# Two-layer mixture behind a windowed attention: a new order for its beginning, and the last accumulator copied and stored in halves

## The chip, the cores and the metric

The kernel runs on one core of a Trainium2 chip. The metric is the device time of one execution in microseconds (us). The core has five engines that run their own instruction streams in order and wait for each other by semaphores: TensorE (PE in the rows, with its weight loads as PEld), VectorE (DVE), ScalarE (ACT), GpSimd (POOL) and SyncE (SP), which here issues every transfer between DRAM and the core's SBUF. Matmuls write to PSUM banks, which VectorE and ScalarE read.

## The reference

Attention in a window of 64 keys feeds a feed-forward layer with a squared ReLU, and that feeds one with x·cos(x).

```python
# q, k, v: (4, 8, 576, 64); moe_*: d_model 512, d_ff 2048; 2304 tokens
scores = scale * np.matmul(q, k.transpose(0, 1, 3, 2))
rel = pos[:, None] - pos[None, :]
scores = np.where((rel >= 0) & (rel < window), scores, -1e9)   # window 64
attn = softmax(scores)                       # exp(s - max) / (sum + 1e-9)
x = np.matmul(attn, v)                       # -> (2304, 512)
h = np.maximum(x @ w_in, 0.0);  x = h * h @ w_out          # first layer, weights w1
h = x @ w_in;                   out = h * np.cos(h) @ w_out   # second layer, weights w2
```

The weights are 8-byte floats. The kernel turns each 1 MB piece of them into a rounded fp32 high part and an fp32 remainder, and makes each matmul of three products (high·high, high·low, low·high).

## The kernel before

**Attention.** The 2304 tokens are nine blocks of 256, the heads two groups of four, so there are 18 attention units, named n_g (block, group). A unit loads `qk` and `v`, makes scores S (line 633, 32 matmuls), masks them and takes their maximum on VectorE (line 650), exponentiates them on ScalarE (line 656), normalises them on VectorE (line 666), transposes them in two halves T on TensorE (line 675), copies the halves to PT (line 301 or 305; `pb` for two units, by ScalarE or VectorE) and multiplies them by v to O (line 690, 32 matmuls). O becomes X, a high and a low part (lines 301, 305, 729).

**First layer.** The weights w1 come in 16 tiles: `raw_in_w1_dram_j` is loaded (line 330), converted by ScalarE (lines 341, 301) and VectorE (lines 353, 357) and split into `W` high (line 301 or 305) and `W` low (line 379, on VectorE or GpSimd). For each tile j, `ph` (line 1193) is 12 matmuls of X with W, `r` is its ReLU (line 772), `g` is r² in two parts (lines 776, 780, 785), and `accA` (lines 799, 860) adds 12 matmuls of g with the second half of W. The first 512 tokens are taken in two passes of 256 (128x256 tiles). `ph_i` runs two places ahead of the `accA` that takes g_i.

**Second layer's weights.** While the first layer runs, w2 tiles `raw_in_w2_dram_j` are loaded by the same line 330, converted to `cw` and from there split and combined into w2o, w2a and w2b, which are stored to DRAM. The second layer (from about 480 us on) reads them back and ends with accumulators `accB` (line 1042), which are copied to `o` (line 1056) and stored (line 1062).

**What sets the order.** Everything is declared as operations with the engines that could do them, a cost on each, a key and dependencies. `Plan.run` is a list scheduler that walks an estimated clock: among operations that could start first, it takes the lowest key, and books the engine. The order of each engine's instructions is that in which the plan took them; what an instruction really waits for is only its data and its buffers, and all behind it on its engine wait too. Keys and engines of the beginning come from the table `START`, searched offline against that estimate: `att` (key and spacing of a unit), `conv` (keys of conversion, split and load of the first nine tiles), `load` (keys of a unit's loads), `cast` and `low` (tiles whose split or low word VectorE may do too), `pool` (tiles whose `W` low GpSimd may do). A transfer costs SyncE in the estimate `max(0.6 * n, nbytes / 360e3)` us, and lands 2.2 us later. Where the plan sees TensorE wait, `keep_busy` puts in matmuls on a constant tile `still` (line 290), which write nothing that is used.

**Rings.** Raw tiles, W and w2 tiles share one ring of 18 slots in SBUF. `qk`, `v` and `PT` have one buffer each, so the next unit's `qk` can be loaded when the S before it is done, and its `v` when the O before it is done. SyncE issues in order, so a load behind these waits with them.

Of the kernel before, what the change touches and what calls it, by code (L numbers as in the profile page):

```python
# [16 lines left out]
P = 128  # L17
# [69 lines left out]
class Plan:  # L87
# [21 lines left out]
    def run(self):  # L109
        engines = sorted({e for o in self.ops for e in o.engs})  # L110
        free = dict.fromkeys(engines, 0.0)
        cand = {e: [] for e in engines}
# [74 lines left out]
def pe_us(n, passes=1):  # L187
# [5 lines left out]
START = {'ahead': 3,  # L193
          'att': {(0, 0): (-45.7, 5.7),
                  (0, 1): (-50.5, 14),
                  (1, 0): (-102.5, 14),
                  (1, 1): (-126.9, 4.1),
                  (2, 0): (7.3, 14),
                  (2, 1): (15.4, 9.4)},
          'cast': (0, 1, 2, 3, 4, 7, 9, 11, 12, 13),  # L200
          'conv': {0: (-8.4, 19.7, -47.8),
                   1: (-25.5, 11.0, -66.1),
                   2: (7.1, -30.3, -8.4),
                   3: (9.9, -33.5, -4.1),
                   4: (4.1, 8.7, -28.0),
                   5: (38.5, -3.6, 19.0),
                   6: (13.2, 7.2, 28.6),
                   7: (59.2, 17.9, -0.6),
                   8: (-4.2, 39.2, 23.5)},
          'diag': (),  # L210
          'exact': 3,
          'halves': 4,
          'load': {(0, 0): (-103.4, -79.0),
                   (0, 1): (-125.7, -51.9),
                   (1, 0): (-45.2, -57.1),
                   (1, 1): (-44.0, -53.5),
                   (2, 0): (19.6, 22.7),
                   (2, 1): (-5.1, 14.4)},
          'low': (0, 4, 5, 7, 9),
          'pool': (0, 1, 5, 6, 7, 9),  # L220
          'upper': ((0, 0), (0, 1), (1, 0), (1, 1), (2, 0), (2, 1))}
# [3 lines left out]
def kernel(  # L225
# [67 lines left out]
    def dma(key, fn, nbytes, deps=(), take=(), use=(), n=1, order=()):  # L293
        return op({"SP": max(0.6 * n, nbytes / 360e3)}, key, fn, [*deps, *order], take, use, lat=2.2)
# [727 lines left out]
    class Job:  # L1022
# [7 lines left out]
        def tile_op(self, m, key):  # L1030
# [22 lines left out]
            def cp_(e):  # L1053
                o["o"] = ma.tile([P, DM], F32, tag="x2", name=f"o_{p}_{half}_{m}")
                if e == "ACT":
                    nc.scalar.activation(o["o"], acc[0], AF.Copy)
                else:
                    nc.vector.tensor_copy(o["o"], acc[0])

            def st(e):  # L1060
                r0 = p * TW + half * H + m * P
                nc.sync.dma_start(out[r0:r0 + P, :], o["o"])
# [362 lines left out]
```

## Time and profile before

| | us |
|---|---|
| median of 3 runs | 857.79 |
| runs | 857.65, 857.79, 859.60 |
| profiled execution, its time | 857.64 |
| its span in the trace | 855.9 |
| outside the span | 1.74 |
| TensorE busy in the span | 843.2 (99%) |
| mean granted clock of TensorE | 0.995 of full speed |

The span is from the first to the last event of the profiled execution. TensorE is the engine with work nearly all the time, so a change of the time is a change of the stretches in which it waits or runs at a lower clock; what the other engines do counts where TensorE waits for it. Names in the trace drop the numbers of a tile: `raw_in_w_dram` is a raw tile of w1 or w2.

### The profile page before, as it was taken

The numbers are of one execution on the slowest core, as the hardware profiler recorded it, in microseconds if no ns is written. First come the engines' busy times: TensorE is split into PE (matmuls) and PEld (weight loads), VectorE is DVE, ScalarE is ACT, GpSimd is POOL, SyncE is SP. The second block draws the span as 40 slices with busy tenths as digits, with TensorE's granted clock in tenths as the row PEclk, the third lists the DMA queues.
The fourth block names the chain that finished last, engine by engine and source line by source line (L and its number), as shares of the span: only waits on it lengthen the run. The fifth ranks groups of instructions, "written<-read, shape, count | busy, mean of one in ns | idle before, by whom it ended". The sixth has DMA issues, their size and how long they took to land.

```text
span 855.9 us, 13984 instructions
## 1 busy us (share of the span) xinstructions
PE 843.2 (99%) x5248; PEld 737.3 (86%) x5248; DVE 574.6 (67%) x1348; ACT 514.0 (60%) x1090; POOL 10.7 (1%) x27
## 2 busy tenths in 40 slices
PE   7899999999999999999999999999999999999998
PEld 6798889998888888888888999988999988999986
DVE  6999666755656557543811688878688886788851
ACT  7799666756656666656433655564555563555542
POOL 3100000000000000000000000000000000000000
PEclk9899999999999999999999999999999999999999
DMA  8782334716445364543941297025453044643010
GB/s 346 309 330 92 103 119 187 288 53 240 188 174 203 142 228 151 177 192 124 337 192 37 86 397 280 13 93 240 183 199 124 1 158 174 231 150 124 1 38 37
DMA packets 28595, 144.16 MB, mean 168 GB/s; under 512 B 3056, under 2 KB 3568, under 8 KB 18288
## 3 DMA queue, kind: packets, MB, share of 16 engines
q1 hardware_dynamic: 28528, 143.27, 44.6%
q8 instruction: 41, 0.67, 0.3%
q14 instruction: 26, 0.21, 0.1%
HBM read 110.76 MB, written 32.51 MB: 167 GB/s over the span
## 4 chain that ended last, share of the span: by engine, by line
PE 94%; DMA 2%; DVE 2%; ACT 1%; issue 0%; POOL 0%; POOLq 0%; ACTq 0%; SPq 0%
PE accB L1042 23%; PE ph L1193 22%; PE accA L799 21%; PE x L1084 12%; PE z L1084 6%; PE y L1084 3%; PE O L690 2%; PE S L633 2%; PE T L675 2%; PE accA L860 1%; DMA w2a_dram<-w2a 1%; ACT pb L656 1%; DMA raw_in_w_dram<-in_w_dram 1%; DVE raw_in_w_dram L357 0%; DVE cw_in_w_dram L353 0%
## 5 line engine op out<-in xcount | busy, mean ns | idle before, releaser
L1193 PE MATMUL ph<-X,W_in_w_dram 128*128 128x512 f32 (+1 forms) x1008 | 215.7, 362 | 0.0
L799 PE MATMUL accA<-g,W_in_w_dram 128*128 128x512 f32 (+1 forms) x912 | 203.8, 370 | 0.0
L1193 PEld LDWEIGHTS ph<-X,W_in_w_dram 128*128 128x128 f32 x1008 | 170.3, 189 | 29.1 <-issue 1.2
L799 PEld LDWEIGHTS accA<-g,W_in_w_dram 128*128 128x128 f32 x912 | 157.7, 189 | 28.5 <-issue 1.5
L785 DVE TENSOR_TENSOR g<-r,g 128x512 fp32r<-128x512 f32 (+1 forms) x84 | 51.5, 614 | 95.2 <-ACT r L780 94.6
L1042 PE MATMUL accB<-wo,gb_e 128*128 128x512 f32 x432 | 100.1, 389 | 0.0
L1042 PEld LDWEIGHTS accB<-wo,gb_e 128*128 128x128 f32 x432 | 81.0, 188 | 16.6
L776 ACT ACTIVATE g<-r 128x512 fp32r<-128x512 f32 (+1 forms) x84 | 47.9, 570 | 73.9 <-PE accA L799 73.2
L772 ACT ACTIVATE r<-ph 128x512 f32<-128x512 f32 (+1 forms) x84 | 44.7, 532 | 42.4 <-PE ph L1193 41.5
L656 ACT ACTIVATE pb<-pb,mm 128x128 f32<-128x128 f32 x144 | 55.8, 390 | 14.9 <-DVE mm L650 14.8
L1042 PE MATMUL accB<-wo,gb_b 128*128 128x512 f32 x216 | 54.3, 393 | 0.0
L1042 PE MATMUL accB<-wo,gb_a 128*128 128x512 f32 x216 | 54.2, 393 | 0.0
L780 ACT ACTIVATE r<-r 128x512 f32<-128x512 f32 (+1 forms) x84 | 48.0, 571 | 2.6
L1042 PEld LDWEIGHTS accB<-wo,gb_b 128*128 128x128 f32 x216 | 40.2, 188 | 7.5
L1100 ACT ACTIVATE held<-x 128x384 f32<-128x384 f32 x72 | 34.4, 481 | 20.3 <-PE x L1084 20.3
L1042 PEld LDWEIGHTS accB<-wo,gb_a 128*128 128x128 f32 x216 | 40.2, 188 | 7.2
L1084 PE MATMUL x<-X,wb 128*128 128x384 f32 x216 | 45.7, 337 | 0.0
L1084 PE MATMUL x<-X,wa 128*128 128x384 f32 x216 | 45.3, 335 | 0.0
L353 DVE TENSOR_SCALAR cw_in_w_dram<-raw_in_w_dram 128x1024 int32<-128x1024 int32 x32 | 23.0, 721 | 30.6 <-ACT raw_in_w_dram L341 30.5
L341 ACT ACTIVATE raw_in_w_dram<-raw_in_w_dram 128x1024 f32<-128x1024 f32 x32 | 36.6, 1146 | 7.1 <-DMA raw_in_w_dram<-in_w_dram 7.1
L1084 PEld LDWEIGHTS x<-X,wa 128*128 128x128 f32 x216 | 38.7, 188 | 2.4
L1084 PEld LDWEIGHTS x<-X,wb 128*128 128x128 f32 x216 | 38.5, 188 | 0.3
(130 smaller groups left out, 1263.6 us busy)
## 6 DMA issues: line engine op xcount, KB each, us to landing
raw_in_w_dram<-in_w_dram SPq DMA_DIRECT2D x32, 1024.0 KB, 7.0
wa<-w2a_dram SPq DMA_DIRECT2D x24, 1024.0 KB, 7.1
wb<-w2b_dram SPq DMA_DIRECT2D x24, 768.0 KB, 5.8
qk<-in_qk_dram SPq DMA_DIRECT2D x17, 576.0 KB, 5.7
v<-in_v_dram SPq DMA_DIRECT2D x18, 512.0 KB, 3.7
w2o_dram<-w2o SPq DMA_DIRECT2D x8, 1024.0 KB, 4.0
w2a_dram<-w2a SPq DMA_DIRECT2D x8, 1024.0 KB, 5.0
wo<-w2o_dram SPq DMA_DIRECT2D x8, 1024.0 KB, 9.8
```

The costliest lines, as they stand in the source:

```text
L341: nc.scalar.activation(hw, hw, AF.Prelu, scale=2.0**-112, alpha=-(2.0**32))
L353: nc.vector.tensor_scalar(s["w"], words()[1], 3, None, ALU.logical_shift_left)
L656: nc.scalar.activation(t["pb"][:, e, r, i], t["pb"][:, e, r, i], AF.Exp, bias=t["mm"][:, e, r, i:i + 1], scale=-1.0, accum_out=t["sm"][:, ...
L772: nc.scalar.activation(t["r"], ph()[:, 0:w], AF.Relu)
L776: nc.scalar.activation(t["g"][:, 0], t["r"], AF.Square)
L780: nc.scalar.activation(t["r"], t["r"], AF.Square)
L785: nc.vector.tensor_tensor(t["g"][:, 1], t["r"], f32(t["g"][:, 0]), ALU.subtract)
L799: nc.tensor.matmul(self.acc[i][:, k, :], w[:, 1, wl, m * P:m * P + P], t["g"][:, gl, :], start=(j == 0 and p == 0 and k == 0 and self.n > ...
L1042: nc.tensor.matmul(acc[0], t["g"][:, gl, m * P:m * P + P], wb.tile[:, k % 2, wl], start=(k == 0 and i == 0), stop=(k == NJ - 1 and i == 2))
L1084: nc.tensor.matmul(ps[x], wb.tile[:, i, wl, c * P:c * P + P], piece(o, c, xl), start=(first and c == 0 and k == 0), stop=(last and c == 1 ...
L1100: return b, op({"ACT": act_us(H)}, key - 6, lambda e: nc.scalar.activation(r_at(b), ps[x], AF.Copy), [dep, o_rooms], [b], [buf], lat=0.39)
L1193: nc.tensor.matmul(t["ph"][:, 0:u.w], wb.tile[:, 0, wl, c * P:c * P + P], u.x(xl, c), start=(c == 0 and k == 0), stop=(c == NCC - 1 and k ...
```

## The change

The table `START` is replaced, with two numbers of the estimate that it was sought with: a load costs `nbytes / 400e3`, and SyncE's first transfer can begin at 0.7 us. Only tables and costs of the plan differ there, no operation of the computation. Work moves between the engines that may do it. The last accumulator `accB` is copied in two halves of 256 columns, one by ScalarE and one by VectorE, and each half is stored by itself; all other accumulators are copied and stored as before. In the new file a line is one further down (three after the last edit).

```diff
@@ class Plan: def run(self):
         free = dict.fromkeys(engines, 0.0)
+        free["SP"] = 0.7
@@ START (a few of its lines)
-          'conv': {0: (-8.4, 19.7, -47.8),
-                   1: (-25.5, 11.0, -66.1),
+          'conv': {0: (-8.3, 25.4, -70.8),
+                   1: (-12.2, -1.3, -83.6),
...
-          'low': (0, 4, 5, 7, 9),
-          'pool': (0, 1, 5, 6, 7, 9),
+          'low': (0, 2, 5, 6, 9),
+          'pool': (0, 1, 3, 5, 7, 11),
@@ def dma
-        return op({"SP": max(0.6 * n, nbytes / 360e3)}, key, fn, [*deps, *order], take, use, lat=2.2)
+        return op({"SP": max(0.6 * n, nbytes / 400e3)}, key, fn, [*deps, *order], take, use, lat=2.2)
@@ second layer, end of an accumulator
-            def cp_(e):
-                o["o"] = ma.tile([P, DM], F32, tag="x2", name=f"o_{p}_{half}_{m}")
-                if e == "ACT":
-                    nc.scalar.activation(o["o"], acc[0], AF.Copy)
-                else:
-                    nc.vector.tensor_copy(o["o"], acc[0])
-
-            def st(e):
+            def cp_(e, at):
+                if at.start == 0:
+                    o["o"] = ma.tile([P, DM], F32, tag="x2", name=f"o_{p}_{half}_{m}")
+                copy(e, o["o"][:, at], acc[0][:, at])
+
+            def st(e, at):
                 r0 = p * TW + half * H + m * P
-                nc.sync.dma_start(out[r0:r0 + P, :], o["o"])
-
-            c = op({"ACT": act_us(DM, False), "DVE": dve_us(DM)}, key - 8.0, cp_, [line[0]], [b],
-                   [acc[1]])
-            dma(key - 8.0, st, P * DM * 4, [c], use=[b])
+                nc.sync.dma_start(out[r0:r0 + P, at], o["o"][:, at])
+
+            end = (p, half, m) == (NPAIR - 1, 1, H // P - 1)
+            for k0, w, e in ((0, DM // 2, "ACT"), (DM // 2, DM // 2, "DVE")) if end else ((0, DM, None),):
+                at = slice(k0, k0 + w)
+                us = {"ACT": act_us(w, False), "DVE": dve_us(w)}
+                c = op({e: us[e]} if e else us, key - 8.0, lambda e, at=at: cp_(e, at), [line[0]],
+                       [] if k0 else [b], [b, acc[1]] if k0 else [acc[1]])
+                dma(key - 8.0, lambda e, at=at: st(e, at), P * w * 4, [c], use=[b])
```

The plan is walked anew as a whole, so the order changes far behind the beginning too: TensorE's order is the same again from about 135 us on, the other engines' keep small exchanges of neighbours up to the second layer. Three places follow.

**VectorE, about 20 us.** From the shift for the first weight tile on; `pb_1_0` is the block whose two transposes TensorE waits for there. Before:

```order
L353 TENSOR_SCALAR cw_in_w1_dram_0_371<-raw_in_w1_dram_0_209 128x1024
L662 TENSOR_SCALAR sm_1_0_353<-sm_1_0_353 128x4
L663 RECIPROCAL sm_1_0_353<-sm_1_0_353 128x4
L666 TENSOR_TENSOR pb_1_0_329<-pb_1_0_329,sm_1_0_353 128x512
L357 ISA raw_in_w1_dram_0_209<-raw_in_w1_dram_0_209,cw_in_w1_dram_0_371 128x1024x2
L662 TENSOR_SCALAR sm_1_0_353<-sm_1_0_353 128x4
L663 RECIPROCAL sm_1_0_353<-sm_1_0_353 128x4
L666 TENSOR_TENSOR pb_1_0_329<-pb_1_0_329,sm_1_0_353 128x512
L353 TENSOR_SCALAR cw_in_w1_dram_2_404<-raw_in_w1_dram_2_306 128x1024
L305 CAST W_in_w1_dram_0_417<-raw_in_w1_dram_0_209 128x2x512
```

In the change:

```order
L354 TENSOR_SCALAR cw_in_w1_dram_0_368<-raw_in_w1_dram_0_193 128x1024
L358 ISA raw_in_w1_dram_0_193<-raw_in_w1_dram_0_193,cw_in_w1_dram_0_368 128x1024x2
L663 TENSOR_SCALAR sm_1_0_353<-sm_1_0_353 128x4
L664 RECIPROCAL sm_1_0_353<-sm_1_0_353 128x4
L667 TENSOR_TENSOR pb_1_0_311<-pb_1_0_311,sm_1_0_353 128x512
L663 TENSOR_SCALAR sm_1_0_353<-sm_1_0_353 128x4
L664 RECIPROCAL sm_1_0_353<-sm_1_0_353 128x4
L667 TENSOR_TENSOR pb_1_0_311<-pb_1_0_311,sm_1_0_353 128x512
L306 COPY PT_1_0_404<-T_1_0_0_386 128x512
L730 TENSOR_TENSOR X_80<-O_0_0_333,X_80 128x2x256
```

Before, the first half of `pb_1_0` is normalised between the two conversions of tile 0 and the second behind them; in the change both conversions stand ahead of both. A PT copy and a low part of X follow, the `low` word of tile 2 comes to VectorE, and the high parts of W of tiles 0 and 2 go to ScalarE.

**SyncE, about 98 us.** From the v of unit 2_1 on. Before:

```order
L609 DMA v_2_1_1208<-in_v_dram 128x1024
L605 DMA qk_3_0_1218<-in_qk_dram 128x1152
L330 DMA raw_in_w2_dram_0_1291<-in_w2_dram 128x2048
L609 DMA v_3_0_1340<-in_v_dram 128x1024
L605 DMA qk_3_1_1349<-in_qk_dram 128x1152
L609 DMA v_3_1_1480<-in_v_dram 128x1024
L605 DMA qk_4_0_1490<-in_qk_dram 128x1152
```

In the change:

```order
L610 DMA v_2_1_1206<-in_v_dram 128x1024
L606 DMA qk_3_0_1215<-in_qk_dram 128x1152
L610 DMA v_3_0_1319<-in_v_dram 128x1024
L606 DMA qk_3_1_1328<-in_qk_dram 128x1152
L331 DMA raw_in_w2_dram_0_1351<-in_w2_dram 128x2048
L610 DMA v_3_1_1457<-in_v_dram 128x1024
L606 DMA qk_4_0_1466<-in_qk_dram 128x1152
```

The first w2 load stood behind qk_3_0 and ahead of v_3_0; now it stands behind v_3_0 and qk_3_1. These two wait for O of unit 2_1 and S of unit 3_0. On VectorE the shift of that tile stands ahead of the copy of the second half of PT_3_0 in both. Before:

```order
L353 TENSOR_SCALAR cw_in_w2_dram_0_1422<-raw_in_w2_dram_0_1291 128x1024
L305 COPY PT_3_0_1399<-T_3_0_1_1425 128x512
L357 ISA cw_in_w2_dram_0_1422<-raw_in_w2_dram_0_1291,cw_in_w2_dram_0_1422 128x2048
L305 CAST w2o_0_1458<-cw_in_w2_dram_0_1422 128x512
L409 TENSOR_TENSOR w2o_0_1458<-cw_in_w2_dram_0_1422,w2o_0_1458 128x512
```

In the change:

```order
L354 TENSOR_SCALAR cw_in_w2_dram_0_1404<-raw_in_w2_dram_0_1351 128x1024
L306 COPY PT_3_0_1378<-T_3_0_1_1399 128x512
L358 ISA cw_in_w2_dram_0_1404<-raw_in_w2_dram_0_1351,cw_in_w2_dram_0_1404 128x2048
L786 TENSOR_TENSOR g_17_1411<-r_17_1386,g_17_1411 128x512
L410 TENSOR_TENSOR w2o_0_1436<-cw_in_w2_dram_0_1404,w2o_0_1436 128x512
```

What moved around it is on TensorE: O of unit 3_0, which reads PT_3_0, stood behind all 12 matmuls of `ph_18` and 12 of `accA`; in the change it stands behind 6 of `ph_18`. O of 2_1 and S of 3_0 also stand earlier, by 9 matmuls of `accA` and 6 of `ph_17`.

**ScalarE, about 242 us.** From the conversion of the seventh w2 tile on. Before:

```order
L341 ACTIVATE raw_in_w2_dram_6_2805<-raw_in_w2_dram_6_2805 128x1024
L776 ACTIVATE g_44_2844<-r_44_2828 128x512
L780 ACTIVATE r_44_2828<-r_44_2828 128x512
L301 ACTIVATE raw_in_w2_dram_6_2805<-raw_in_w2_dram_6_2805 128x1024
L772 ACTIVATE r_45_2865<-ph_45_2840 128x512
L301 ACTIVATE PT_6_0_2809<-T_6_0_1_2860 128x512
L301 ACTIVATE X_80<-O_6_0_2878 128x2x256
```

In the change:

```order
L342 ACTIVATE raw_in_w2_dram_6_2796<-raw_in_w2_dram_6_2796 128x1024
L302 ACTIVATE raw_in_w2_dram_6_2796<-raw_in_w2_dram_6_2796 128x1024
L777 ACTIVATE g_44_2851<-r_44_2829 128x512
L781 ACTIVATE r_44_2829<-r_44_2829 128x512
L302 ACTIVATE w2o_3_2862<-cw_in_w2_dram_6_2842 128x512
L773 ACTIVATE r_45_2870<-ph_45_2844 128x512
L302 ACTIVATE PT_6_0_2810<-T_6_0_1_2864 128x512
L302 ACTIVATE X_80<-O_6_0_2879 128x2x256
```

The second conversion (line 302 of the change, raw from raw) now stands ahead of the two squares, and a copy of `cw_in_w2_dram_6` to w2o, which VectorE did before, stands ahead of the ReLU and the copy of PT_6_0.

## Rows read from the trace of the kernel before

**Rows 1.** Page: busy time, share of the span, instructions of an engine
```profile
PE 843.2 (99%) x5248; PEld 737.3 (86%) x5248; DVE 574.6 (67%) x1348; ACT 514.0 (60%) x1090; POOL 10.7 (1%) x27
```

**Rows 2.** Windows: busy (x) PE, PEld, DVE, ACT, POOL; clock, DMA share, GB/s
```profile
25.00:30.00 5.00, 4.43 (x49) 3.86 (x51) 4.90 (x7) 3.95 (x5) 2.72 (x1) 0.53 1.01 422
30.00:35.00 5.00, 5.00 (x57) 4.67 (x58) 4.96 (x20) 2.27 (x12) 0.61 (x1) 0.79 0.95 353
```

**Rows 3.** Timeline of TensorE, 20 to 38: start, duration, instruction, idle before
```profile
23.98 0.63 PE L675 MATMUL T<-ident,pb 128*128 128x128 f32 x4 [2.99 <-DVE pb L666]
...
26.14 1.08 PE L675 MATMUL T<-ident,pb 128*128 128x128 f32 x4 [0.57 <-DVE pb L666]
...
31.83 4.64 PE L1193 MATMUL ph<-X,W_in_w_dram 128*128 128x256 f32 x33
```

**Rows 4.** Timeline of GpSimd, 14 to 45
```profile
19.86 2.40 POOL L379 TENSOR_TENSOR W_in_w_dram<-raw_in_w_dram,W_in_w_dram 128x1024 fp32r<-128x1024 f32 x1 [13.32 <-ACT W_in_w_dram L301]
27.28 3.34 POOL L379 TENSOR_TENSOR W_in_w_dram<-raw_in_w_dram,W_in_w_dram 128x1024 fp32r<-128x1024 f32 x1 [5.01 <-DVE W_in_w_dram L305]
```

**Rows 5.** Timeline of VectorE, 14 to 45
```profile
21.18 1.64 DVE L353 TENSOR_SCALAR cw_in_w_dram<-raw_in_w_dram 128x1024 int32<-128x1024 int32 x1
...
25.91 0.69 DVE L353 TENSOR_SCALAR cw_in_w_dram<-raw_in_w_dram 128x1024 int32<-128x1024 int32 x1
...
28.37 2.80 DVE L305 CAST W_in_w_dram<-raw_in_w_dram 128x1024 fp32r<-128x1024 f32 x1
...
34.09 1.22 DVE L379 TENSOR_TENSOR W_in_w_dram<-raw_in_w_dram,W_in_w_dram 128x1024 fp32r<-128x1024 f32 x1
```

**Rows 6.** Timeline of SyncE's queue, 94 to 127
```profile
98.57 0.33 SPq L605 DMA_DIRECT2D qk<-in_qk_dram  x1
99.01 0.37 SPq L330 DMA_DIRECT2D raw_in_w_dram<-in_w_dram  x1
```

**Rows 7.** Line 330, loads issued from 95 to 260: issue to landing
```profile
DMA to landing us min/median/max: 4.7/7.1/8.4
```

**Rows 8.** Line 330, the load issued at 99.01: issue to landing
```profile
DMA to landing us min/median/max: 7.9/7.9/7.9
```

**Rows 9.** Timeline of TensorE, 94 to 124
```profile
109.56 1.10 PE L633 MATMUL S<-qk 64*64 64x128 f32 x32
...
112.08 2.90 PE L799 MATMUL accA<-g,W_in_w_dram 128*128 128x512 f32 x12
114.83 0.85 PE L1193 MATMUL ph<-X,W_in_w_dram 128*128 128x512 f32 x3
...
121.34 1.15 PE L690 MATMUL O<-PT,v 128*64 128x64 f32 x32
```

**Rows 10.** Timeline of VectorE, 108 to 123
```profile
120.05 0.69 DVE L305 COPY PT<-T 128x512 f32<-128x512 f32 x1 [0.76 <-PE T L675]
```

**Rows 11.** Timeline of ScalarE, 227 to 250
```profile
242.11 1.11 ACT L341 ACTIVATE raw_in_w_dram<-raw_in_w_dram 128x1024 f32<-128x1024 f32 x1 [2.98 <-DMA raw_in_w_dram<-in_w_dram]
...
244.31 1.12 ACT L301 ACTIVATE raw_in_w_dram<-raw_in_w_dram 128x1024 int32<-128x1024 uint32 x1
245.33 0.58 ACT L772 ACTIVATE r<-ph 128x512 f32<-128x512 f32 x1
245.81 0.58 ACT L301 ACTIVATE PT<-T 128x512 f32<-128x512 f32 x1
```

**Rows 12.** Timeline of VectorE, 227 to 250
```profile
245.47 1.22 DVE L357 CUSTOM_DVE_ANT_0 cw_in_w_dram<-raw_in_w_dram,cw_in_w_dram 128x2048 uint16<-128x2048 uint16 x1 [0.34 <-ACT raw_in_w_dram L301]
```

**Rows 13.** Timeline of TensorE, 227 to 250
```profile
246.45 1.15 PE L690 MATMUL O<-PT,v 128*64 128x64 f32 x30 [0.41 <-ACT PT L301]
```

**Rows 14.** Timeline of ScalarE, 849 to 858, the last copy
```profile
852.04 0.60 ACT L1056 ACTIVATE o<-accB 128x512 f32<-128x512 f32 x1 [1.49 <-PE accB L1042]
```

**Rows 15.** Line 1062, output stores issued from 845 on: issue to landing
```profile
DMA to landing us min/median/max: 2.0/2.0/2.3
```

**Rows 16.** Groups of ScalarE by form: busy, mean ns, idle before
```profile
L772 ACT ACTIVATE r<-ph 128x256 f32<-128x256 f32 x24 | 9.0, 376 | 3.5 <-PE ph L1193 2.7
```

More of the change, by code (lines that the diff above doesn't have):

```diff
@@ L188, in pe_us @@
     return max(0.108, 0.0134 + passes * n / 2400.0)
[L193 to L200, printed above, removed]
-          'conv': {0: (-8.4, 19.7, -47.8),
-                   1: (-25.5, 11.0, -66.1),
[L203 to L209, printed above, removed]
+START = {'ahead': 2,
+          'att': {(0, 0): (-23.1, 3.5),
+                  (0, 1): (-45.9, 14),
+                  (1, 0): (-116.4, 11.4),
+                  (1, 1): (-122.9, 14),
+                  (2, 0): (8.8, 12.4),
+                  (2, 1): (-6.3, 3.4)},
+          'cast': (3, 4, 6, 7, 9, 11, 14, 15),
+          'conv': {0: (-8.3, 25.4, -70.8),
+                   1: (-12.2, -1.3, -83.6),
+                   2: (0.8, -25.1, 1.9),
+                   3: (-1.3, -49.8, 5.6),
+                   4: (1.7, -4.9, -37.5),
+                   5: (38.9, 3.3, 27.3),
+                   6: (7.9, 9.0, 40.8),
+                   7: (62.6, 22.0, -5.5),
+                   8: (10.3, 36.0, 37.5)},
           'diag': (),
-          'exact': 3,
+          'exact': 5,
           'halves': 4,
[L213 to L218, printed above, removed]
-          'low': (0, 4, 5, 7, 9),
-          'pool': (0, 1, 5, 6, 7, 9),
-          'upper': ((0, 0), (0, 1), (1, 0), (1, 1), (2, 0), (2, 1))}
+          'load': {(0, 0): (-89.2, -90.6),
+                   (0, 1): (-140.3, -61.5),
+                   (1, 0): (-44.6, -41.1),
+                   (1, 1): (-39.2, -32.9),
+                   (2, 0): (8.8, 25.6),
+                   (2, 1): (6.3, 22.5)},
+          'low': (0, 2, 5, 6, 9),
+          'pool': (0, 1, 3, 5, 7, 11),
+          'upper': ((0, 1), (1, 0), (2, 0))}
 @with_exitstack
```

## The prediction

> **What bounds the kernel now.** The page comes first: TensorE is busy 843.2 of 855.9 us [rows 1], so at most some 13 us can be won, and anything that makes TensorE wait is paid in full. The windows of the beginning come next, since the list of TensorE's waits has all but one of them ahead of 31 us: there one sees the granted clock at 0.53 of full speed (its lower level, 1.2 GHz) from 25 to 30 and 0.79 as a mean from 30 to 35, while VectorE is busy 4.90 and 4.96 of 5 us [rows 2]. TensorE's timeline shows why it idled before: 2.99 us until the first transpose of unit 1_0, then again until the second at 26.14, both for a normalisation on VectorE; from 31.83 on it has work [rows 3]. So in the beginning VectorE sets the pace, and the clock fell behind the idle stretch. Behind that I read each place where the order differs, on the timelines of the engine that waits and of the one it waits for. One wait is left there, 0.41 us at 246.45 for a copy of PT by ScalarE [rows 13].
>
> **The beginning (term: -0.3 us).** VectorE had two operations of 0.69 us and more that took far longer than their like. The shift at 21.18 took 1.64 us against 0.69 for the one at 25.91, and the high part of W at 28.37 took 2.80 [rows 5]. Both lie beside GpSimd's low parts of W, 19.86 to 22.26 and 27.28 to 30.62 [rows 4], and both end 0.55 us behind them: VectorE's operation seems to run only when GpSimd's has ended. In the change, the two operations on X of unit 0_0 leave their place ahead of the masks, so the shift of tile 0 can begin at 21.18 - 2 x 0.6 = 20.0. But W low of tile 1 stays on GpSimd at about 19.7 to 22.1, so the shift ends at about 22.7 as before; and now the add of tile 0 (1.22, as in [rows 12]) stands ahead of the first normalisation. That one, with its two small steps of 0.4, ends at 24.9 and the second at 25.9. The first transpose moves from 23.98 to 25.0, the second from 26.14 to 26.0. TensorE idles 4.0 instead of 2.99 us, and the second transpose, which matters for O of 1_0, gains 0.1.
> Behind it VectorE had 0.6 + 0.6 + 1.2 + 2.8 us from 25.9 to the high part of X of 1_0 at 31.1. Now it has a copy of PT and a low part of X (0.6 each, from PSUM), the low word of tile 2 from about 27.2, which waits for GpSimd's W low of tile 0 to end (it can begin when ScalarE has W high, about 25.6, and takes 2.4: until 28.1, so the low word ends at 28.7), then shift and add of tile 2: 30.5. The chain that follows (X, eight masks, W low of tile 2 at 34.09 [rows 5], normalisations, transposes) is 0.6 earlier. TensorE's own chain at the lower clock (transpose, O, S, then 24 matmuls) is only 0.1 to 0.2 earlier. The gain is between the two, 0.15 to 0.6; I take 0.3. Bounds: 0.9 of gain if VectorE and GpSimd run beside each other; 0.4 of loss if the half clock slows what now stands behind a later transpose.
>
> **The first w2 load (term: +1.1 us).** Before, it was issued at 99.01, 0.44 behind qk_3_0 [rows 6], and landed 7.9 us later [rows 8], long before ScalarE read it. In the change it stands behind v_3_0 and qk_3_1, and qk_3_1 waits until S of 3_0 has read the only `qk` buffer. That S began at 109.56; 15 matmuls that stood ahead of it now follow. Twelve take 114.83 - 112.08 = 2.75 us with what lies between, or 0.23 each [rows 9], so S begins at 106.1, ends 1.1 later, qk_3_1 is issued at 107.3 and the w2 load at 107.7. Loads from here to 260 us landed in 4.7 to 8.4 us [rows 7]; with a v and a qk issued just ahead, as here, it was 7.9 [rows 8] or more. That gives 115.6 to 116.1. Then come ScalarE's conversion (1.1, as at 242.11 [rows 11]), VectorE's shift (0.7) and, queued behind the shift, the copy of the second half of PT_3_0 (0.69 [rows 10]): done at 118.1 to 118.6.
> O of 3_0 needs that copy. It began at 121.34, 10.7 us behind the end of S of 3_0 [rows 9], with 42 matmuls and two transposes between; now there are 39, which makes 10.0, so TensorE comes to it at 117.2. It waits 0.9 to 1.4 us: 1.1. Nothing covers this, since all of TensorE's later work is queued behind O. Bounds: no wait at all for a landing within 7.0 us, 1.4 at the slow end.
>
> **The seventh w2 tile (term: +0.8 us).** ScalarE converted at 242.11, then made two squares, the second conversion at 244.31, the ReLU at 245.33 and the copy of PT, which ended at 246.39 [rows 11]; O began behind it [rows 13]. The load of this tile depends on the same semaphores in both orders, so it should land where it did. In the change the second conversion goes from 243.1 to 244.25, VectorE's add behind it (1.22 [rows 12]) to 245.5, and ScalarE, which has its squares done by then, waits for the add, since the copy to w2o reads it. That copy costs 0.55, the ReLU 0.5, the copy of PT 0.58: 247.2 instead of 246.4. The add was beside this chain before and is now in it. So 0.8 us, bounds 0.6 and 1.0, and nothing if the tile lands over 1.3 us earlier.
>
> **Other moves (term: 0).** The first scores begin some 0.45 later behind two more pairs of constant matmuls, but ScalarE, whose exponentials set the pace there, has one copy less ahead of its first conversion, so that starts at the same time. The loads that are swapped at 260 us and later read buffers that are free earlier than TensorE wants them; W of tiles 5 and 8 is ready about 1 us before it is used. This 1 us is all their cover.
>
> **The tail (term: -0.1 us).** The last copy took 0.60 [rows 14]. ScalarE copies 256 columns in 0.376 [rows 16] while VectorE does the other half. The first store can go 0.2 earlier; the second follows on SyncE 0.44 behind (the distance of two issues in [rows 6]), so 0.2 later than the one store before. A store landed in 2.0 to 2.3 us [rows 15]. If half the bytes take as long, that is 0.2 lost; at 422 GB/s [rows 2] the half saved is 0.3 of flow, which gives 0.1 gained. I take 0.1 gained, bounds +0.25 and -0.3.
> [...]
>
> **Sum.** 857.64 - 0.3 + 1.1 + 0.8 - 0.1 = 859.1 us, against the profiled execution's own time, which is 0.15 below the median of the runs shown. About 2.6 us (0.3%) can be told from no change here, so this is no measurable change, on the slow side.
>
> **Rivals.** (1) The first w2 load lands in time, as the load with 4.7 us did: 858.0. For it speaks that the median is 7.1; against it the v and qk just ahead. (2) The beginning gets slower, and with it the kernel: the transpose comes 1 us later, the idle stretch is longer, and TensorE runs at the lower level for about 5 us more; at 0.53 that is 0.47 x 5 = 2.3 us, 861.4 in all. It decides from 1.3 us on, that is from 2.7 us more at the lower level. For it speaks that the clock fell behind an idle stretch of 2.99; against it that VectorE covers part of the loss. The Trainium skill, TensorE: Matmul & The Clock Gate, section What's actually happening, puts an idle engine back to 1.2 GHz; the trace agrees (0.53 behind the idle stretch [rows 2]). (3) The beginning gains much more: VectorE's operations aren't held by GpSimd, and TensorE keeps its full clock. The excess of the two long operations is 0.95 + 2.1 = 3.0 us, so at most that much goes: 859.1 + 0.3 - 3.0 = 856.4, and 855.3 if the load lands in time too. Against it speaks that both ended 0.55 us behind GpSimd's. (4) All the moves are covered: neither new wait shows, 857.2.
>
> **How the numbers follow.** Forecast 0.45 (own range 858.2 to 860.2), (1) 0.2, (2) 0.2, (3) 0.08, (4) 0.07. Slower by over 0.3% needs 860.4: nearly all of (2) and the slow edge of the forecast, 0.24. Faster needs 855.2: (3) with the load in time and the tail at its good end, 0.05. The rest is 0.71. The range runs from 856.8, between (3) and (4), to 861.2, short of the full price of (2).
>
> **What would show it.** VectorE's shift of tile 0 should begin near 20.0 and take over 2 us; TensorE's idle stretch before unit 1_0 should be about 4 us; the w2 load should be issued near 107.7 and TensorE wait about 1.1 us for VectorE's copy of PT at O of 3_0, and 1.2 for ScalarE's at O of 6_0 instead of 0.41. I am wrong if these waits are missing, if the windows up to 35 us show another clock, or if a wait stands at a place that I called covered.

## The result and the profile after

The changed kernel takes 862.95 us (median of 6 runs, 859.23 to 864.87) beside 858.25 for the kernel before (6 runs, 857.59 to 859.60): a ratio of 1.0051, 95% interval 1.0027 to 1.0074. It is slower by 0.5%, where I had forecast 859.1 us and no measurable change, with 861.2 as the upper end of the range. (Medians here and below are of all runs; ratios and their intervals leave out four slow runs of 929 to 3400 us and are not the quotients of the medians.) The profiled execution took 863.49 us (its span is 861.7), 5.85 more than the one profiled before, where the medians differ by 4.70. What follows explains those two executions; how far others repeat it is told with the experiments.

The busy times of TensorE and ScalarE are those of before to 0.1 us [rows 1], so the loss lies in waits.

```profile
PE 843.3 (98%) x5250; PEld 737.6 (86%) x5250; DVE 573.2 (67%) x1345; ACT 514.1 (60%) x1094; POOL 9.8 (1%) x27
```

The list of TensorE's waits (line, what it waited for, us in total, times, longest) names them. The second and third rows are to be looked at first: a second transpose that I had placed 0.1 us earlier than before waits 2.4, and O waits for ScalarE's copies of PT at two places, not at one.

```profile
PE T L676 <- DVE sm L663: 4.2, 2, 3.5
PE T L676 <- DVE pb L667: 2.8, 2, 2.4
PE O L691 <- ACT PT L302: 2.6, 2, 1.8
...
PE O L691 <- DVE PT L306: 0.7, 1, 0.7
```

**The beginning.** The timeline of TensorE, in the order of [rows 3]: matmuls of constants, first scores, the two transposes of unit 1_0, its O, and the first `accA`, the mark by which I measure the beginning.

```profile
1.19 4.89 PE L291 MATMUL S<-still 128*128 128x128 f32 x22 [1.19 <-DVE still L286]
6.01 1.54 PE L634 MATMUL S<-qk 64*64 64x128 f32 x48
...
20.45 1.61 PE L291 MATMUL T<-still 128*128 128x128 f32 x13 [0.59 <-issue]
25.53 0.63 PE L676 MATMUL T<-ident,pb 128*128 128x128 f32 x4 [3.47 <-DVE sm L663]
...
28.76 1.09 PE L676 MATMUL T<-ident,pb 128*128 128x128 f32 x4 [2.37 <-DVE pb L667]
...
31.06 1.98 PE L691 MATMUL O<-PT,v 128*64 128x64 f32 x32
...
39.89 1.31 PE L861 MATMUL accA<-g,W_in_w_dram 128*128 128x256 f32 x9
```

The same marks in the kernel before, of which no row was shown:

```profile
1.19 4.00 PE L290 MATMUL S<-still 128*128 128x128 f32 x18 [1.19 <-DVE still L285]
5.12 1.54 PE L633 MATMUL S<-qk 64*64 64x128 f32 x48
...
37.87 1.31 PE L860 MATMUL accA<-g,W_in_w_dram 128*128 128x256 f32 x9
```

The first `accA` is 2.02 us later. The first of the two waits is no surprise (I had said 4 us of idling; it is 3.47, and 0.59 more between the matmuls on constants ahead of it). The second is, and the timelines of VectorE and GpSimd of the changed kernel, which answer to [rows 4, 5], show what it is:

```profile
20.39 2.71 DVE L354 TENSOR_SCALAR cw_in_w_dram<-raw_in_w_dram 128x1024 int32<-128x1024 int32 x1
...
24.70 0.69 DVE L667 TENSOR_TENSOR pb<-pb,sm 128x512 f32<-128x512 f32 x1
...
25.71 2.90 DVE L667 TENSOR_TENSOR pb<-pb,sm 128x512 f32<-128x512 f32 x1
...
29.74 0.68 DVE L308 TENSOR_SCALAR raw_in_w_dram<-raw_in_w_dram 128x1024 int32<-128x1024 uint32 x1
```

```profile
20.15 2.41 POOL L380 TENSOR_TENSOR W_in_w_dram<-raw_in_w_dram,W_in_w_dram 128x1024 fp32r<-128x1024 f32 x1 [13.57 <-DMA v<-in_v_dram]
25.68 2.40 POOL L380 TENSOR_TENSOR W_in_w_dram<-raw_in_w_dram,W_in_w_dram 128x1024 fp32r<-128x1024 f32 x1 [3.11 <-ACT W_in_w_dram L302]
```

GpSimd's second low part of W begins at 25.68, the second normalisation at 25.71. The normalisation, 0.69 us of work, ends 0.53 behind GpSimd, as the shift ahead of it ends 0.54 behind the first low part. I had expected the operation held there to be the low word at 29.74; it came through in 0.68. In the kernel before, the second normalisation had no low part of GpSimd beside it:

```profile
25.30 0.69 DVE L666 TENSOR_TENSOR pb<-pb,sm 128x512 f32<-128x512 f32 x1
```

**O of three units.** On TensorE's timeline each O now comes in two pieces: two matmuls, then the wait for the copy of the second half of PT, then 30. At the first and second of these places the kernel before had no such wait ([rows 9], and the first row below); at the third it had 0.41 [rows 13]. At the second it had the copy of PT on VectorE. Before:

```profile
206.39 1.15 PE L690 MATMUL O<-PT,v 128*64 128x64 f32 x32
```

```profile
205.10 0.69 DVE L305 COPY PT<-T 128x512 f32<-128x512 f32 x1 [1.08 <-PE T L675]
```

In the change:

```profile
119.30 0.33 PE L691 MATMUL O<-PT,v 128*64 128x64 f32 x2
120.37 1.15 PE L691 MATMUL O<-PT,v 128*64 128x64 f32 x30 [0.74 <-DVE PT L306]
...
209.72 0.33 PE L691 MATMUL O<-PT,v 128*64 128x64 f32 x2
210.86 1.15 PE L691 MATMUL O<-PT,v 128*64 128x64 f32 x30 [0.81 <-ACT PT L302]
...
250.15 0.33 PE L691 MATMUL O<-PT,v 128*64 128x64 f32 x2
252.26 1.15 PE L691 MATMUL O<-PT,v 128*64 128x64 f32 x30 [1.78 <-ACT PT L302]
```

What a wait displaces is the distance of the two pieces less about 0.07 for two matmuls: 1.0 at unit 3_0, 1.07 at 5_0, 2.04 at 6_0, of which 0.67 stood there before, so 1.37. With the beginning that is 2.02 + 1.0 + 1.07 + 1.37 = 5.46 of the 5.85. The rest, 0.4, I did not place; 0.3 of it is there by O of 5_0, to which TensorE comes 3.33 us later than before (209.72 instead of 206.39).

ScalarE's timeline answers to [rows 11]. At unit 5_0 the copy of PT stands behind both conversions of the fifth w2 tile, whose load landed at 207.66 (the first row waited for it). At unit 6_0 it stands behind both conversions, two squares and the copy to w2o.

```profile
207.67 1.13 ACT L342 ACTIVATE raw_in_w_dram<-raw_in_w_dram 128x1024 f32<-128x1024 f32 x1 [1.04 <-DMA raw_in_w_dram<-in_w_dram]
208.70 1.13 ACT L302 ACTIVATE raw_in_w_dram<-raw_in_w_dram 128x1024 int32<-128x1024 uint32 x1
...
210.19 0.61 ACT L302 ACTIVATE PT<-T 128x512 f32<-128x512 f32 x1
...
247.14 1.13 ACT L342 ACTIVATE raw_in_w_dram<-raw_in_w_dram 128x1024 f32<-128x1024 f32 x1 [3.56 <-DMA raw_in_w_dram<-in_w_dram]
...
250.61 0.63 ACT L302 ACTIVATE w2o<-cw_in_w_dram 128x512 fp32r<-128x512 f32 x1
...
251.62 0.59 ACT L302 ACTIVATE PT<-T 128x512 f32<-128x512 f32 x1
```

**The tail.** The chain of waits, at its end, has ScalarE's half and VectorE's half one behind the other, not side by side:

```profile
857.87 0.39 ACT o L302
858.26 0.02 issue
858.28 0.42 DVE o L306
```

From the start of ScalarE's copy to the end of the span it is 861.7 - 857.87 = 3.83 us, and before 855.9 - 852.04 = 3.86 [rows 14]. In this pair of executions the tail gains 0.03 us.

### The profile page after: what moved, and what is told of

Read it like the earlier page. It is cut to its first block, busy times and chain, and to the rows that moved or that the text cites. A ratio compares the mean times of both kernels' runs of the same rounds, so it can differ in the third digit from the quotient of the medians.

```text
span 861.7 us, 13997 instructions
## 1 busy us (share of the span) xinstructions
PE 843.3 (98%) x5250; PEld 737.6 (86%) x5250; DVE 573.2 (67%) x1345; ACT 514.1 (60%) x1094; POOL 9.8 (1%) x27
## 4 chain that ended last, share of the span: by engine, by line
PE 92%; DMA 3%; ACT 2%; DVE 2%; issue 0%; SPq 0%; ACTq 0%
PE accB L1043 23%; PE ph L1196 21%; PE accA L800 20%; PE x L1087 12%; PE z L1087 6%; PE y L1087 3%; DMA raw_in_w_dram<-in_w_dram 2%; PE O L691 2%; PE S L634 2%; PE T L676 1%; PE accA L861 1%; DMA w2a_dram<-w2a 1%; ACT pb L657 1%; PE S L291 1%; DVE pb L667 0%
```

## The experiments

Theory 1 after this reading: the loss is the order's alone, and consists of four places: the second normalisation of unit 1_0 that runs beside GpSimd's low part (called the collision below), and the copies of PT at O of 3_0, 5_0 and 6_0. Theory 2, its rival, is named with each run. In the diffs below `behind(a, b, ...)` takes b, ... out of the written order and puts them right behind a, and `before` right ahead of it; nothing else of the plan changes. All times are medians, beside the kernel before run with them (857.70 us for the first four, 858.27 for shift32, gps_wait2, best_after and best_before, 858.40 for gps_look, 857.94 for nine_first, best_after9 and best_before7).

**order_only.** The changed kernel with the tail of before.

```diff
-                copy(e, o["o"][:, at], acc[0][:, at])
+                if e == "ACT":
+                    nc.scalar.activation(o["o"], acc[0], AF.Copy)
+                else:
+                    nc.vector.tensor_copy(o["o"], acc[0])
...
-                nc.sync.dma_start(out[r0:r0 + P, at], o["o"][:, at])
+                nc.sync.dma_start(out[r0:r0 + P, :], o["o"])
```

> The new table and the two new costs alone; the last accumulator is copied and stored whole, as before. Theory 1 (the loss is made by the new order, in the beginning and at three copies of PT): within 1 us of the change, about 863, and the same waits of TensorE in its trace: about 6.5 us in all for transposes ahead of 31 us, 0.7 at 120, 0.8 at 211 and 1.8 at 252. Theory 2 (the two halves of the tail cost something by themselves): about 858 to 860, nearer to the kernel before.

Measured: 862.70 us, ratio 1.0047 (1.0027 to 1.0067). The order alone makes the loss; the halves of the tail neither add nor save what can be told.

Its trace doesn't repeat all the sizes that I expected. The waits at O of 3_0 and 5_0 are 0.68 and 0.89, but the one at 6_0 is 0.67, not 1.8. A further one of 1.22 stands at 173 us, for a ReLU on ScalarE behind the two conversions of a w2 tile, whose load ScalarE waited for 2.43 us there and 0.74 in the profiled changed kernel:

```profile
173.23 1.70 PE L1194 MATMUL ph<-X,W_in_w_dram 128*128 128x256 f32 x12 [1.22 <-ACT r L773]
...
253.97 1.15 PE L691 MATMUL O<-PT,v 128*64 128x64 f32 x30 [0.67 <-ACT PT L302]
```

In the five traces of the new order that leave the three places as they are (the changed kernel, called after here and in the table below, order_only, gps_wait, gps_look, nine_first) TensorE idles 0 to 0.74 us at O of 3_0, 0 to 0.95 at 5_0 and 0.67 to 2.31 at 6_0. So the three sizes above are those of one execution.

**waits_off.** The changed kernel with three moves back: the first w2 load ahead of v_3_0, and at the fifth and seventh w2 tile the second conversion and the add (with the copy to w2o at the seventh) behind the copy of PT. (In the names, `c1` is the second conversion, `add` VectorE's add behind it, `w2o` and `w2ol` the copy to w2o and its low part; the last number of a PT is its half.)

```diff
+        before(("v", 3, 0), ("load", "in_w2_dram_0"))
+        behind(("PT", 5, 0, 1), ("c1", "in_w2_dram_4"), ("add", "in_w2_dram_4"))
+        behind(("PT", 6, 0, 1), ("c1", "in_w2_dram_6"), ("add", "in_w2_dram_6"), ("w2o", 3, 0), ("w2ol", 3, 0))
```

> The change, with three operations moved in the written order: the first w2 load stands ahead of v_3_0 again; the copies of PT_5_0 and PT_6_0 on ScalarE stand ahead of the second conversion of their w2 tile, and of the copy to w2o. Theory 1 (each of the three waits is made by that order): TensorE's waits at 120, 211 and 252 are gone or under 0.3 us each, and the time falls by about 3.4, to 860. Theory 2 (late w2 transfers make them, whatever the order behind them): the first wait goes, the other two stay at half or more, about 861.5.

Measured: 859.60 us, ratio 1.0014 (1.0004 to 1.0025), 3.35 below the changed kernel and 3.1 below order_only, with which it ran. The three places were moved together, so what each is worth by itself was not measured. The list of TensorE's waits of this run ends with the beginning; no O waits any more, while the wait for the normalisation stays:

```profile
PE T L702 <- DVE sm L689: 5.0, 2, 4.3
PE T L702 <- DVE pb L693: 2.4, 2, 2.0
PE S L660 <- DVE mm L677: 2.0, 1, 2.0
PE S L311 <- DVE still L306: 1.2, 1, 1.2
```

**gps_wait.** GpSimd waits with its low part of tile 0 until the second normalisation is done, by a copy of 8 columns of its result to a new small tile.

```diff
+    hold = cp.tile([P, 8], F32, name="hold")
...
+            if j == 0 and e == "POOL":
+                nc.gpsimd.tensor_copy(hold[:, 0:8], watch["pb"])
```

> The change, with one edit: GpSimd reads 8 columns of the second normalised half of pb_1_0 ahead of its low part of W of tile 0, so that this part starts behind that normalisation instead of 0.03 us ahead of it. Theory 1 (VectorE's operations from SBUF to SBUF wait while GpSimd computes a low part): the normalisation takes 0.7 instead of 2.90, the second transpose comes near 26.5 instead of 28.76, and the time falls by about 2, to 861. Theory 2 (VectorE is held by the transfers, which run at full rate there): the normalisation stays long, no change. Theory 3 (the lower clock makes the loss, not the wait): the transpose comes earlier, but the first accA still starts at 39.5 or later.

Measured: 866.49 us, ratio 1.0095 (1.0080 to 1.0110): slower than the changed kernel, not faster. The beginning alone did what theory 1 says. On VectorE's timeline the normalisation is short again, and the operation that is held now is the low word, which has time:

```profile
25.70 0.69 DVE L695 TENSOR_TENSOR pb<-pb,sm 128x512 f32<-128x512 f32 x1
...
27.51 2.14 DVE L326 TENSOR_SCALAR raw_in_w_dram<-raw_in_w_dram 128x1024 int32<-128x1024 uint32 x1
```

The second transpose came at 26.54 instead of 28.76 and the first `accA` at 38.22 instead of 39.89. Then the gain was lost all along the first layer: twelve matmuls to `ph` of 512 columns took 2.96 us there, 2.88 to 2.91 in the changed kernel. The new tile had moved all later ones of the pool by 32 bytes.

**all_fixed.** waits_off and gps_wait together, with a tile of its own for each half of the last output.

```diff
+                o[at.start] = ma.tile([P, DM], F32, tag="x2", name=f"o_{p}_{half}_{m}_{at.start}")
+                copy(e, o[at.start][:, at], acc[0][:, at])
```

> The change with the edits of both other runs, and with a tile of its own for each half of the last accumulator, so that the second copy need not wait for the first. Theory 1: all the losses found are gone: 0.3 gained in the beginning, 0.4 at the wait that the kernel before had at 246, 0.4 in the tail, so 856.8 against 857.6 for the kernel before. Theory 2 (something not seen yet costs time): 858 or more.

Measured: 863.15 us, ratio 1.0055 (1.0040 to 1.0070). It has the same shift of 32 bytes in it, so its time says nothing against theory 1; its beginning repeats gps_wait's (first `accA` at 38.34). VectorE's half still began 0.23 behind the end of ScalarE's, now waiting for an earlier store from its buffer, so whether the halves can run side by side was not shown.

**shift32.** The kernel before with an unused tile of 32 bytes.

```diff
     still = cp.tile([P, 2, P], F32, name="still")
+    cp.tile([P, 8], F32, name="spare")
```

> The kernel before with a tile of 32 bytes a partition that nothing uses, ahead of the weights' ring in SBUF. No instruction is added or moved. Theory 1 (matmuls of the first layer run slower when their operands are moved by 32 bytes): 12 matmuls of ph take 2.80 instead of 2.72 us and the time is 4 to 5 us more, about 862. Theory 2: no change, 857.7.

Measured: 862.43 us, ratio 1.0044 (1.0028 to 1.0060). The groups of TensorE by form (busy us, mean ns) put most of it at the matmuls to `ph` of 512 columns. The kernel before, then shift32:

```profile
L1193 PE MATMUL ph<-X,W_in_w_dram 128*128 128x512 f32 x720 | 176.1, 392 | 0.0
```

```profile
L1194 PE MATMUL ph<-X,W_in_w_dram 128*128 128x512 f32 x720 | 179.8, 397 | 0.0
```

That is 3.7 beside the 4.2 us by which the medians differ; of the second layer's `accB` one group grew by 1.5 and another shrank by 0.7. An experiment that adds a tile must put it where nothing moves.

**gps_wait2** and **gps_look.** gps_wait with the 8 columns copied to a small tile that the kernel has already, so that nothing moves. gps_look is the same kernel, traced once more.

```diff
-    edge.tile([P, 8], F32, name="edge")
+    hold, watch = edge.tile([P, 8], F32, name="edge"), {}
```

> The same edit of the change as in gps_wait (GpSimd's W low of tile 0 behind the second normalisation of pb_1_0), but its 8 columns go to a small tile that was there already, so that no other tile moves in SBUF. Theory 1 (VectorE waits for GpSimd; the loss of gps_wait came from the 32 bytes by which its new tile moved the tiles behind it): the normalisation takes 0.7, the first accA starts near 38.2, 12 matmuls of ph take 2.72 us again, and the time is about 861.5. Theory 2 (the later W low itself made the rest slower): 865 or more again.

> The same kernel as gps_wait2, whose one trace showed a whole execution at the lower clock and can't be read. Theory 1 (the collision of the second normalisation of unit 1_0 with GpSimd's low part of W delays the beginning; the price of the 32 bytes is separate): normalisation at 25.7 of 0.69 us, second transpose at about 26.5 instead of 28.76, first accA at about 38.2 instead of 39.89, twelve ph in 2.88 (not 2.96), time 861 to 862, about 1 us below the changed kernel. Theory 2 (the beginning is late for another reason, later dummies or the clock): first accA still at 39.5 or later though the transpose comes early.

Measured: gps_wait2 861.99 us, ratio 1.0037 (1.0020 to 1.0054); gps_look 861.23, ratio 1.0032 (1.0021 to 1.0043). So the wait of GpSimd gains 1.0 to 1.7 us on the changed kernel by the medians, but the intervals overlap that of the changed kernel (1.0027 to 1.0074), so the times alone do not decide. The trace of gps_look seems to speak for theory 2, with the first `accA` at 39.95. But all of its beginning stands 0.7 us or more later from the first exponential on (8.30 instead of 7.59), and the windows show the lower clock in a stretch where the profiled changed kernel had none. (Columns as in [rows 2].)

```profile
10.00:15.00 5.00, 4.37 (x37) 4.12 (x38) 3.88 (x21) 4.80 (x24) 0.00 (x0) 0.66 1.00 390
```

From there on I compared all traces by three marks, read from their timelines:

| kernel | first exponential | first `accA` | between | clock 10 to 15 us | collision |
|---|---|---|---|---|---|
| before | 6.70 | 37.87 | 31.17 | 1.00 | |
| shift32 | 7.19 | 38.36 | 31.17 | 1.00 | |
| after | 7.59 | 39.89 | 32.30 | 1.00 | yes |
| waits_off | 7.25 | 39.47 | 32.22 | 1.00 | yes |
| gps_wait | 7.59 | 38.22 | 30.63 | 1.00 | no |
| all_fixed | 7.70 | 38.34 | 30.64 | 1.00 | no |
| order_only | 8.07 | 41.21 | 33.14 | 0.66 | yes |
| gps_look | 8.30 | 39.95 | 31.65 | 0.66 | no |
| best_after | 8.18 | 39.77 | 31.59 | 0.66 | no |

Behind the first exponential the beginning is as good as fixed. The collision costs 1.6 to 1.7 us at the full clock (32.22 and 32.30 against 30.63 and 30.64) and 1.5 at the lower (33.14 against 31.65 and 31.59). Without it the new order is 31.17 - 30.63 = 0.54 faster than the old one. The lower clock at 10 to 15 us goes with 0.8 to 1.0 more in this distance, and comes in some executions of the old order too (0.67 and 0.71 in the last two kernels below). And the first exponential itself comes later in the new order (7.25 to 8.30, against 6.70 and 7.19).

**best_after.** order_only with gps_wait2 and waits_off: the new order without the four places.

> The new table and costs with the tail of before, with the edits of gps_wait2 and waits_off, so without the three waits and without the collision at the normalisation. Theory 1 (these four are the whole loss): 857.5 to 858, level with the kernel before, because the new beginning then ends 0.3 later than the old one (38.2 against 37.87 for the first accA) and 0.6 is won at the wait that the kernel before has at 246. Theory 2 (the new table also costs elsewhere): 859 or more.

Measured: 858.39 us, ratio 0.9999 (0.9985 to 1.0013), level with the kernel before. The four places make the whole loss, to about 1 us. (This kernel also lacks the 0.7 us that the kernel before loses at O of 6_0 [rows 13], so the rest of the new order may still cost about that much.) Its profiled execution is its slowest (861.88), and the wait at 172 us that order_only had is 2.19 in it:

```profile
171.83 1.69 PE L1225 MATMUL ph<-X,W_in_w_dram 128*128 128x256 f32 x12 [2.19 <-ACT r L804]
```

The kernel before and the profiled changed kernel have no wait there. So a w2 load that lands later makes part of the difference between executions of one kernel.

**nine_first** and **best_after9.** The first scores stand behind 11 matmuls of constants, where the order before had 9 (22 and 18 rows above). Back to 9, in the changed kernel and in best_after:

```diff
+        next(o for _, o in order if o.pre).pre = 9
```

> The changed kernel with 9 matmuls of constants ahead of its first scores, as before the change, instead of 11. In the traces so far the first exponential of the new order stands at 7.25 to 8.30 us, that of the old at 6.70 to 7.46, and from there to the first accA it is a fixed distance (31.17 in the old order, 32.2 to 32.3 in the new at full clock). Theory 1: the two matmuls delay the scores, and all of the beginning with them: first scores at 5.1 to 5.4 instead of 6.01, first exponential at 6.7 to 7.2, and the kernel is 0.7 to 0.8 us faster, 862.2. Theory 2: the scores wait for the load of qk in either case, or something behind them gives the time back: no change, 862.9.

> The new order without its three later waits and without the collision at unit 1_0 (best_after, which was level with before), now with 9 matmuls of constants ahead of the first scores instead of 11. Theory 1: 0.7 to 0.8 us faster than best_after, 857.6, ratio about 0.999; from the first exponential to the first accA 30.6 us at full clock. Theory 2: no change, 858.4.

Measured: nine_first 860.78 us, ratio 1.0031 (1.0019 to 1.0043), but best_after9 858.33, ratio 1.0001 (0.9992 to 1.0010). The first is more than I expected, with an interval that overlaps the changed kernel's; the second is nothing. In both traces the scores began at 5.33 as expected, but took 2.0 us instead of 1.54, so the first exponential came at 7.41 and 7.39. The clock was at 0.68 from 10 to 15 us, and from the first exponential on they agree with the table's rows for that clock: 33.26 us to the first `accA` with the collision, 31.65 without it. What two matmuls of constants cost in the end stays open.

**best_before** and **best_before7.** The kernel before with what was learnt: GpSimd's low part of tile 0 waits for VectorE's high part of tile 2, and the copy of PT of 6_0 goes ahead of the second conversion, the add and the copy to w2o; then the same with 7 matmuls of constants first.

```diff
+        behind(("Whi", 2), ("Wlo", 0))
+        behind(("PT", 6, 0, 1), ("c1", "in_w2_dram_6"), ("add", "in_w2_dram_6"), ("w2o", 3, 0), ("w2ol", 3, 0))
...
+            if j == 0 and e == "POOL":
+                nc.gpsimd.tensor_copy(hold, f32(watch["w"]))
```

> The kernel before with two edits of the same kind: GpSimd's W low of tile 0 waits until VectorE has made W high of tile 2, and the copy of PT_6_0 on ScalarE stands ahead of the second conversion of its w2 tile. Theory 1 (VectorE waits for GpSimd there too): W high of tile 2 takes 0.7 instead of 2.80, the high part of X of 1_0 comes near 30 instead of 31.09; TensorE gains only 0.2 of it, since the lower clock holds it there, and 0.6 at O of 6_0: 856.9. Theory 2 (the W low of tile 0 comes too late for ph_0): 858 or more.

> best_before with 7 matmuls of constants ahead of the first scores instead of 9. Theory 1 at its end: if qk has landed by then the first scores begin at about 4.7 and the kernel is 0.4 to 0.8 us faster, 856.5, ratio 0.997. Theory 2: TensorE then waits for qk as long as it saved, or works with fewer matmuls at the lower clock: 857.1 or more.

Measured: best_before 857.14 us, ratio 0.9978 (0.9963 to 0.9993); best_before7 857.10, ratio 0.9987 (0.9974 to 1.0000). They are the fastest kernels here, by about 1 us, which is less than the 0.3% that I called measurable, and the second interval reaches 1. VectorE's cast of 2.80 us [rows 5] now takes 0.70 (timeline of best_before), but TensorE waits 1.7 for the low part that was put off, so most of the gain is given back:

```profile
29.43 0.70 DVE L324 CAST W_in_w_dram<-raw_in_w_dram 128x1024 fp32r<-128x1024 f32 x1
```

```profile
PE ph L1223 <- POOL W_in_w_dram L404: 1.7, 1, 1.7
```

Two matmuls fewer gave nothing more: the first scores began at 4.64, and the next ones then waited 2.6 us for their qk.

## Why the prediction was wrong

The terms of the sum make +1.5 us, and the two profiled executions differ by 5.85. Of the 4.35 missed, 2.3 lie in the beginning, 1.1 at the fifth w2 tile, 0.6 at the seventh, and the rest in what is not placed.

**The beginning (-0.3 forecast, +2.02 measured) is the step that failed.** I had the mechanism: VectorE's operation ends 0.55 us behind GpSimd's if they lie beside each other. I had the moment: GpSimd "can begin when ScalarE has W high, about 25.6". And I had the first normalisation at 24.9, so the second at 25.9. But I applied the rule only to the low word behind it, and let the second normalisation, which stands at the same moment, through at 0.69 us. Two estimates 0.3 us apart, both wrong by more than the 0.03 that decided, can't tell which of two operations comes first; I should have priced both cases. Nor was it an accident of one execution: in all four traces with the collision (after, waits_off, order_only, nine_first) GpSimd begins 0.00 to 0.05 ahead. The case that happened costs 1.6 us by the table, and holds the transposes, where mine would have held an operation with time to spare (gps_wait: 2.14 us for the low word, and the earliest `accA` of the new order).

The trace before held the other case too, which the prediction does not use. GpSimd's second low part took 3.34 us [rows 4], where the first took 2.40; it began 0.17 behind VectorE's add, which kept its usual 1.22:

```profile
27.11 1.22 DVE L357 CUSTOM_DVE_ANT_0 raw_in_w_dram<-raw_in_w_dram,cw_in_w_dram 128x2048 uint16<-128x2048 uint16 x1
```

In these rows whichever begins first goes on; my rule, that VectorE's operation waits for GpSimd's, was half of it.

The Trainium skill, SBUF — State Buffer, section SBUF: two separate sides, states the rule behind these rows: VectorE and GpSimd share a pair of ports, which VectorE uses in its two-port modes, and for an operation with two SBUF inputs against one of GpSimd that reads SBUF; the one that starts first keeps the pair for the whole instruction while the other is blocked. The trace agrees: 2.90 us for 0.69 of work with two inputs, started 0.03 behind.

The gain that I did expect is real: without the collision the new order is 0.54 us shorter from the first exponential on, within my 0.15 to 0.6. It was covered by a second miss. I counted the two added pairs of constant matmuls at 0.45 us and as free, because ScalarE's first conversion would start at the same time. The scores began 0.89 later (11 took 4.89 us, 9 took 4.00, so it is 0.45 for each in these two executions; in the other traces 11 took 4.54 to 5.06 and 9 took 4.21), the first exponential 0.89 later, and the conversion 0.41 later (14.24 instead of 13.83): one copy less ahead of it made up for only 0.48 of that. So 0.89 + 1.67 - 0.54 makes the 2.02, where 1.67 is 32.30 - 30.63. Whether that lateness is in the time too is open: nine_first speaks for it, best_after9 against it.

Rival (2) had the sign and about the size, "TensorE runs at the lower level for about 5 us more", but not the cause. The windows of the changed kernel show 0.62 and 0.69 of full speed where before they showed 0.53 and 0.79 [rows 2], in sum no longer at the lower level:

```profile
25.00:30.00 5.00, 2.10 (x12) 1.96 (x13) 4.93 (x7) 0.71 (x2) 2.40 (x1) 0.62 1.03 427
30.00:35.00 5.00, 5.00 (x78) 4.49 (x77) 4.12 (x10) 3.91 (x5) 0.00 (x0) 0.69 0.37 123
```

shift32 kept its full clock from 25 to 35 us, and its beginning was no shorter (31.17 in the table): VectorE and GpSimd set the pace, as I had said.

**The first w2 load (+1.1 forecast, +1.0 measured) was right in each step.** The load was issued at 109.80, which is the 107.7 of the forecast and the 2.0 of the beginning, landed 8.0 us later, and O waited for the copy behind VectorE's shift. Rival (1), the load in time, is out for this execution; in the traces of the new order the wait was 0 (gps_wait) to 0.74.

**The seventh w2 tile (+0.8 forecast, +1.37 measured): right mechanism, wrong size.** The chain on ScalarE is the one that I wrote down, conversion, squares, w2o, ReLU, PT. But I let the load land where it did, by the argument that it depends on the same semaphores. It was issued at 241.00 instead of 235.91, 5.09 later, where TensorE was only 4.44 late (250.15 for the first O matmuls instead of 245.71). That 0.65 is the difference. SyncE's own waits show where it comes from: in both orders this load waited for the store of `w2a` ahead of it to land. Before, then in the change:

```profile
SPq L330 <- DMA w2a_dram<-w2a: 5.5, 1, 5.5
```

```profile
SPq L331 <- DMA w2a_dram<-w2a: 6.1, 1, 6.1
```

The store was issued 4.45 us later (233.19 instead of 228.74), just as late as TensorE, but it took 7.8 us to land instead of 7.1. So the semaphores were the same, as I had argued, and the landing was not. The 1.2 of idling that I forecast lies within the 0.67 to 2.31 of the five traces; 1.78 is this execution's.

**The fifth w2 tile (0 forecast, +1.07 measured) was missed.** It lay under "other moves", with a cover of 1 us for all of them, and it is the sign that I had named, a wait at a place that I called covered. The copy of PT of 5_0 had gone from VectorE to ScalarE behind two conversions, the pattern that I priced at the seventh tile. In addition the load took 7.2 us to land, where the one before took 5.9; both lie within the 4.7 to 8.4 of [rows 7]. With loads that vary by that much, a cover of 1 us behind a load is none.

**The tail (-0.1 forecast, 0.0 measured).** The step that failed is that VectorE copies its half "while" ScalarE does the other. It began 0.02 behind ScalarE's end. The Trainium skill, PSUM — Partial Sum Buffer, section PSUM bank collisions raise a hardware error, says that two engines must not access one bank in the same partitions at once, reads included, and that the compiler adds a dependency. Both halves lie in one accumulator, and the row agrees. But both halves are also written to one tile `o`, which could order them by itself; all_fixed, where each half had a tile and another wait came in, does not settle which of the two it is.

## What to carry to other kernels

Where two engines exclude each other, and the order between them is decided by less than the estimate's error, price both orders and see which operation is held in each: here 0.03 us decided over 1.6. When one place of a pattern is found (a copy that TensorE waits for, put behind work that waits for a load), look for all places of it before calling the rest covered. A wait behind a load has the size of the execution that it is read from: at O of 6_0 it was 0.67 in one and 2.31 in another. And an experiment that adds even a small tile should put it where no other tile moves.

## What the runs showed of the hardware

An unused tile of 32 bytes a partition made 720 matmuls slower by 1% (392 to 397 ns each, 176.1 to 179.8 us in all), with the same instructions and the same order; which operand's address does it, and why, stays open. The clock between 10 and 15 us was full in some executions and 0.66 to 0.71 in others, in both orders; in the new order it goes with 0.8 to 1.0 us more up to the first `accA`. What it costs in the whole time was not measured. GpSimd's low part did not hold every operation of VectorE: in gps_wait, with GpSimd busy from 26.68 to 29.09, the low part of X that reads PSUM began at 26.91 and took its usual 0.68 us, and only the low word behind it, from SBUF to SBUF, took 2.14.
